# One matmul fewer for the sum of phi(k): a fold on GpSimd, and one more FFN chunk in the output banks

## The chip, the cores and the metric

The kernel runs on one core of one Trainium2 chip. The metric is the device time of one execution in microseconds (us). A time below is a median of several executions, all of them with a granted TensorE clock of 0.998 to 1.000. The span of a profile is some 1.7 us shorter than the time that is reported for the same execution.

Engines are called as in the profile: PE is TensorE, PEld its weight loads, DVE VectorE, ACT ScalarE, POOL GpSimd, SP the queue that issues the DMAs.

## The reference

A gate mixes a linear-attention block (A) and a SwiGLU block (B) of the same tokens. 2048 tokens, width 512, 32 heads of 16, FFN width 1376, bf16 inputs and output.

```python
def _A_ref(x, wqkv, wo):
    ...                                            # q, k, v: 32 heads of 16
    phi = lambda t: jnp.where(t > 0, t + 1, jnp.exp(t)) + 1e-6
    pq, pk = phi(q), phi(k)
    kv = jnp.einsum("bhsd,bhse->bhde", pk, v)
    z = jnp.einsum("bhsd->bhd", pk)                # the sum of phi(k) over the tokens
    num = jnp.einsum("bhqd,bhde->bhqe", pq, kv)
    den = jnp.einsum("bhqd,bhd->bhq", pq, z)[..., None] + 1e-6
    o = num / den
    return ... @ wo
...
g = _sigmoid((x * gate_w).sum(-1, keepdims=True))
return g * a + (1 - g) * b                         # b = (silu(x w1) * (x w3)) w2
```

The change touches `z`: 512 numbers, each a sum over 2048 tokens, which the kernel needs on all 128 partitions.

## The kernel before

Tokens lie on the partitions, 128 at a time, in 16 tiles. For each tile of k the kernel forms phi(k) and GpSimd adds it to `pks` (128x512, fp32), so that `pks` holds 128 partial sums per column. What remains is to sum over the partitions and to give the result to all of them. A matmul with a matrix of ones does both. Its inputs are bf16, so GpSimd first splits `pks` into a high bf16 part and a low one (what the rounding to bf16 left over), and two products add up in one bank.

```python
    nc.gpsimd.tensor_add(pks[:], pks[:], pk_sb[:, t, :])        # 15 times (L194)
    ...
    for tt in range(TPB - 1):                                   # q of block 0, and the last XP products
        emit_q(0, tt, psM, "mm")
        emit_xp(n_xp + tt, XP_ps)
    ...                                                         # XP_sb copies, last q, rem, kvT
    pks_hi = consts.tile([P, D], BF16, name="pks_hi")
    nc.gpsimd.tensor_copy(pks_hi[:], pks[:])                    # L421
    pks_lo = consts.tile([P, D], BF16, name="pks_lo")
    nc.gpsimd.tensor_sub(pks_lo[:], pks[:], pks_hi[:])          # L423
    for fc in range(FC):
        emit_ffn(0, fc)
        if fc == 0:
            z_ps = psX.tile([P, D], FP32, tag="XP1", name="z_ps")
            nc.tensor.matmul(z_ps[:], lhsT=ones_b[:], rhs=pks_hi[:], start=True, stop=False)   # L428
            nc.tensor.matmul(z_ps[:], lhsT=ones_b[:], rhs=pks_lo[:], start=False, stop=True)   # L429
            nc.scalar.activation(out=z_sb[:], in_=z_ps[:], func=ACT.Copy)
        if 1 <= fc <= TPB:
            emit_den(0, fc - 1)                                 # GpSimd: qz = pq * z_sb (L225)
        ...
```

PSUM has two pools: `psM`, a ring of four banks that nearly everything uses, and `psX`, four single banks XP0 to XP3. An FFN chunk takes two banks of the ring, one for gate and one for up. Chunk 4 of block 0 already goes aside to XP2 and XP3.

```python
    def emit_ffn(tb, fc):
        ...
        aside = tb == 0 and fc == 4
        gate_ps = (psX if aside else psM).tile([P, TB], FP32, tag="XP2" if aside else "mm", ...)
        ...  # four products L310
        up_ps = (psX if aside else psM).tile([P, TB], FP32, tag="XP3" if aside else "mm", ...)
        ...  # four products L318, then ACT tanh, DVE gs (L325), DVE hT (L328)

    def phi(dst, ps):
        e_ins = nc.scalar.activation(out=e[:], in_=ps, func=ACT.Exp)              # L140
        nc.vector.tensor_scalar(out=em[:], in0=e[:], scalar1=1.0, scalar2=1e-6,
                                op0=ALU.min, op1=ALU.add)                         # L142 phi_m
        nc.vector.scalar_tensor_tensor(out=dst, in0=ps, scalar=0.0, in1=em[:],
                                       op0=ALU.max, op1=ALU.add)                  # L145
```

The order of the instructions on PE is fixed by the program.

## Time and profile before

| | before |
|---|---|
| time, first 3 runs | 180.53 us (180.15 to 180.85) |
| span of the profile | 178.7 us |
| PE busy | 174.1 us, 97% |
| DVE, ACT, POOL busy | 67%, 37%, 34% |

The head of the page of the kernel before: span, busy time by engine, and the first line of the chain that ended last.

```profile
span 178.7 us, 2472 instructions
...
PE 174.1 (97%) x877; PEld 84.6 (47%) x893; DVE 119.3 (67%) x205; ACT 66.6 (37%) x126; POOL 61.3 (34%) x69
...
PE 97%; issue 1%; DVE 0%; DVEq 0%
```

A busy PE may still wait between products, so its waits count for more. This is the whole list of PE's waits in the kernel before (who waited for whom: us in total, times, longest):

```profile
PE warm L161 <- PEq L471: 0.8, 1, 0.8
```

One wait, at the start. Now PE around the place of the change, from the timeline of the kernel before (start, duration, engine, line, operation). A line is a group; its duration runs to the end of its last product.

```profile
39.94 0.81 PE L318 MATMUL up_ps<-xT,w_sb 128*128 128x512 bf16 x3
40.59 0.38 PE L428 MATMUL z_ps<-pks_hi,ones_b 128*128 128x512 bf16 x1
40.80 0.38 PE L429 MATMUL z_ps<-pks_lo,ones_b 128*128 128x512 bf16 x1
41.02 1.03 PE L310 MATMUL gate_ps<-xT,w_sb 128*128 128x512 bf16 x4
41.88 1.03 PE L318 MATMUL up_ps<-xT,w_sb 128*128 128x512 bf16 x4
```

The durations are 0.38 us a product, the starts are 0.22 us apart: 40.59, 40.80, 41.02. The products overlap in the pipeline, and the spacing of the starts is what one of them costs in a stream. The same view on POOL and on DVE (idle time and its releaser in brackets):

```profile
34.49 0.61 POOL L421 CAST pks_hi<-pks 128x512 bf16<-128x512 f32 x1
35.18 1.16 POOL L423 TENSOR_TENSOR pks_lo<-pks,pks_hi 128x512 bf16<-128x512 f32 x1
38.95 1.05 POOL L254 TENSOR_TENSOR hr<-upr,gsr 128x192 bf16<-128x192 f32 x2 [2.61 <-DVE cl L258]
41.89 4.54 POOL L225 TENSOR_TENSOR qz<-pq,z_sb 128x512 f32<-128x512 bf16 x4 [1.89 <-ACT z_sb L430]
```

```profile
37.61 0.28 DVE L142 TENSOR_SCALAR phi_m<-phi_e 128x512 bf16<-128x512 bf16 x1
37.92 0.69 DVE L145 SCALAR_TENSOR_TENSOR pq<-q_ps,phi_m 128x512 bf16<-128x512 f32 x1
...
43.09 0.69 DVE L228 TENSOR_REDUCE den<-qz 128x32 f32<-128x512 f32 x1 [1.05 <-POOL qz L225]
```

POOL has split `pks` by 36.34 (35.18 + 1.16), four microseconds before z is due, and then waits for DVE. DVE shows no such wait until 42.04 (the end of the instruction that is cut here), and then waits 1.05 us, until 43.09.

### The profile page before, as it was taken

What the parts mean: (1) busy time and instruction counts of PE and PEld (TensorE: products, weight loads), DVE (VectorE), ACT (ScalarE), POOL (GpSimd) and SP (SyncE); (2) the same over time, 40 slices, a digit from 0 to 9 for tenths busy, and PEclk for the clock granted to TensorE, in tenths of its full rate; (3) what the DMA queues carried; (4) which work ended last, traced back from release to release, by engine and by line L of the source; (5) the groups of instructions that cost most, each with busy time, mean ns of one, the idle gap of its engine ahead of it and who ended that gap; (6) DMA issues with size and microseconds to landing.
All of it is one profiled execution on the core that took longest, in us unless ns stands there. A gap on an engine that the chain in (4) does not pass through costs nothing.

```text
span 178.7 us, 2472 instructions
## 1 busy us (share of the span) xinstructions
PE 174.1 (97%) x877; PEld 84.6 (47%) x893; DVE 119.3 (67%) x205; ACT 66.6 (37%) x126; POOL 61.3 (34%) x69
## 2 busy tenths in 40 slices
PE   8999999999999999999999999999999999999993
PEld 4444444474444545444454544444545444444463
DVE  1588867997998837398786375978754669776000
ACT  3642323476533333342433333342433323341221
POOL 5187575736353323262003232620032328100000
PEclk9999999999999999999999999999999999999999
DMA  5999999901005010124000111240001023300011
GB/s 178 263 272 245 267 321 369 321 6 28 9 12 107 0 48 29 44 55 92 0 4 6 38 37 37 59 93 2 0 7 59 14 62 64 61 0 0 29 44 50
DMA packets 29085, 14.88 MB, mean 83 GB/s; under 512 B 19632, under 2 KB 28816, under 8 KB 29072
## 3 DMA queue, kind: packets, MB, share of 16 engines
q1 hardware_dynamic: 28800, 14.46, 30.2%
q10 hardware_dynamic: 272, 0.26, 0.5%
q8 instruction: 7, 0.11, 0.3%
q14 instruction: 6, 0.05, 0.1%
HBM read 8.42 MB, written 2.10 MB: 59 GB/s over the span
## 4 chain that ended last, share of the span: by engine, by line
PE 97%; issue 1%; DVE 0%; DVEq 0%
PE o_ps L355 19%; PE gate_ps L310 19%; PE up_ps L318 19%; PE o_ps L346 8%; PE q_ps L217 8%; PE XP L204 8%; PE k_ps L184 6%; PE r_ps L241 3%; PE k L184 2%; PE o_ps L350 2%; PE warm L161 2%; PE xTp L174 1%; PE kvT_ps L411 1%; PE W_ps L438 0%; DVE o_out L364 0%
## 5 line engine op out<-in xcount | busy, mean ns | idle before, releaser
L310 PE MATMUL gate_ps<-xT,w_sb 128*128 128x512 bf16 x156 | 40.7, 379 | 0.2
L318 PE MATMUL up_ps<-xT,w_sb 128*128 128x512 bf16 x156 | 40.5, 379 | 0.2
L225 POOL TENSOR_TENSOR qz<-pq,z_sb 128x512 f32<-128x512 bf16 x16 | 18.5, 1165 | 60.3 <-DVE pq L145 58.4
L323 ACT ACTIVATE th<-gate_ps 128x512 bf16<-128x512 f32 x40 | 23.9, 597 | 38.1 <-PE gate_ps L310 36.6
L355 PE MATMUL o_ps<-w_sb,hT 128*128 128x512 bf16 (+2 forms) x176 | 37.3, 354 | 0.2
L325 DVE SCALAR_TENSOR_TENSOR gs<-th,gate_ps 128x512 bf16<-128x512 bf16 x40 | 27.3, 684 | 5.8 <-ACT th L323 5.3
L328 DVE TENSOR_TENSOR hT<-up_ps,gs 128x512 bf16<-128x512 f32 x40 | 27.6, 691 | 3.8
L142 DVE TENSOR_SCALAR phi_m<-phi_e 128x512 bf16<-128x512 bf16 x32 | 15.2, 475 | 18.9 <-ACT phi_e L140 18.8
L355 PEld LDWEIGHTS <-hT 128*128 128x128 bf16 x180 | 16.8, 97 | 17.9
L318 PEld LDWEIGHTS <-w_sb 128*128 128x128 bf16 x160 | 15.6, 98 | 18.9
L310 PEld LDWEIGHTS <-w_sb 128*128 128x128 bf16 x160 | 15.6, 98 | 18.7
L360 ACT ACTIVATE o_out<-o_ps,omg 128x512 bf16<-128x512 f32 (+2 forms) x17 | 11.2, 656 | 30.4 <-PE o_ps L355 30.4
L290 POOL TENSOR_TENSOR pqn<-pq,rden 128x512 bf16<-128x512 bf16 x16 | 16.6, 1057 | 14.0 <-DVE rden L283 11.7
L194 POOL TENSOR_TENSOR pks<-pks,pk_sb 128x512 f32<-128x512 f32 x15 | 17.3, 1155 | 8.1 <-DVE pk_sb L145 7.5
L228 DVE TENSOR_REDUCE den<-qz 128x32 f32<-128x512 f32 x16 | 11.0, 684 | 9.0 <-POOL qz L225 8.9
L346 PE MATMUL o_ps<-W_sb,pqT 128*128 128x512 bf16 (+2 forms) x71 | 16.5, 355 | 0.1
L217 PE MATMUL q_ps<-wq_sb,xT 128*128 128x512 bf16 x63 | 16.4, 379 | 0.1
L204 PE MATMUL XP<-pk_sb,x_sb 128*128 128x512 bf16 x62 | 16.0, 379 | 0.1
L140 ACT ACTIVATE phi_e<-k_ps 128x512 bf16<-128x512 f32 x12 | 7.2, 597 | 14.4 <-PE k_ps L184 12.2
L140 ACT ACTIVATE phi_e<-q_ps 128x512 bf16<-128x512 f32 x16 | 9.6, 597 | 7.8 <-PE q_ps L217 6.7
L184 PE MATMUL k_ps<-wk_sb,xT 128*128 128x512 bf16 x48 | 12.3, 379 | 0.1
L145 DVE SCALAR_TENSOR_TENSOR pq<-q_ps,phi_m 128x512 bf16<-128x512 f32 x16 | 11.1, 691 | 0.5
(59 smaller groups left out, 119.5 us busy)
## 6 DMA issues: line engine op xcount, KB each, us to landing
w_sb<-in_B_w_dram SPq DMA_DIRECT2D x6, 640.0 KB, 8.5
out_dram<-o_out SPq DMA_DIRECT2D x15, 128.0 KB, 1.7
x_sb<-in_A_x_dram SPq DMA_DIRECT2D x3, 512.0 KB, 4.4
x_sb<-in_A_x_dram SPq DMA_DIRECT2D x2, 256.0 KB, 3.5
wq_sb<-in_A_wqkv_dram SPq DMA_DIRECT2D x1, 512.0 KB, 6.6
wv_sb<-in_A_wqkv_dram SPq DMA_DIRECT2D x1, 512.0 KB, 6.5
wo_sb<-in_A_wo_dram SPq DMA_DIRECT2D x1, 512.0 KB, 9.5
wk_sb<-in_A_wqkv_dram ACTq DMA_DIRECT2D x1, 256.0 KB, 3.7
```

What stands on the lines that cost most here:

```text
L184: nc.tensor.matmul(k_ps[:], lhsT=xT[:, kc, t * P : (t + 1) * P], rhs=wk_sb[:, kc, :], start=(kc == 0), stop=(kc == KC - 1),)
L194: nc.gpsimd.tensor_add(pks[:], pks[:], pk_sb[:, t, :])
L204: nc.tensor.matmul(XP_ps[dc][:], lhsT=x_sb[:, t, dc * P : (dc + 1) * P], rhs=pk_sb[:, t, :], start=(t == 0), stop=(t == NT - 1),)
L217: nc.tensor.matmul(q_ps[:], lhsT=xT[:, kc, ts_tok], rhs=wq_sb[:, kc, :], start=(kc == 0), stop=(kc == KC - 1),)
L225: nc.gpsimd.tensor_tensor(out=qz[:], in0=st[tb, "pq"][:, tt, :], in1=z_sb[:], op=ALU.mult)
L310: nc.tensor.matmul(gate_ps[:], lhsT=w1_sb[:, kc, fsl], rhs=xT[:, kc, tok_sl], start=(kc == 0), stop=(kc == KC - 1),)
L318: nc.tensor.matmul(up_ps[:], lhsT=w3_sb[:, kc, fsl], rhs=xT[:, kc, tok_sl], start=(kc == 0), stop=(kc == KC - 1),)
L323: nc.scalar.activation(out=th[:], in_=gate_ps[:], func=ACT.Tanh, scale=0.5)
L325: nc.vector.scalar_tensor_tensor(out=gs[:], in0=th[:], scalar=1.0, in1=gate_ps[:], op0=ALU.add, op1=ALU.mult)
L328: nc.vector.tensor_tensor(out=st[tb, "hT"][:, fc, :], in0=up_ps[:], in1=gs[:], op=ALU.mult)
L346: nc.tensor.matmul(o_ps[:], lhsT=st[tb, "pqT"][:, c, tsl], rhs=W_sb[:, c, a:b], start=(c == 0), stop=False,)
L355: nc.tensor.matmul(o_ps[:], lhsT=st[tb, "hT"][:, fc, tsl], rhs=w2_sb[:, fc, a:b], start=False, stop=(fc == FC - 1),)
```

## The change

The intent is one product for z in place of two. GpSimd adds partitions 64-127 of `pks` onto 0-63. That leaves 64 rows, and the 128 rows of one product hold both parts: the high parts on partitions 0-63, the low parts on 64-127. The fold is emitted earlier in the program than the split was. The second part moves chunk 6 of block 0 out of the ring, to XP0 and XP1, to loosen the ring for a DVE that may be later.

```diff
-        aside = tb == 0 and fc == 4
+        aside = {4: ("XP2", "XP3"), 6: ("XP0", "XP1")}.get(fc) if tb == 0 else None
         gate_ps = (psX if aside else psM).tile(
-            [P, TB], FP32, tag="XP2" if aside else "mm", name="gate_ps"
+            [P, TB], FP32, tag=aside[0] if aside else "mm", name="gate_ps"
         )
 ...                                   # the same for up_ps with aside[1]
         emit_xp(n_xp + tt, XP_ps)
+    HP = P // 2
+    pks_up = consts.tile([HP, D], FP32, name="pks_up")
+    nc.gpsimd.tensor_copy(pks_up[:], pks[HP:P, :])
+    nc.gpsimd.tensor_add(pks[0:HP, :], pks[0:HP, :], pks_up[:])
+    pks_hl = consts.tile([P, D], BF16, name="pks_hl")
+    nc.gpsimd.tensor_copy(pks_hl[0:HP, :], pks[0:HP, :])
+    nc.gpsimd.tensor_sub(pks_hl[HP:P, :], pks[0:HP, :], pks_hl[0:HP, :])
 ...
-    pks_hi = consts.tile([P, D], BF16, name="pks_hi")
-    nc.gpsimd.tensor_copy(pks_hi[:], pks[:])
-    pks_lo = consts.tile([P, D], BF16, name="pks_lo")
-    nc.gpsimd.tensor_sub(pks_lo[:], pks[:], pks_hi[:])
 ...
-            nc.tensor.matmul(z_ps[:], lhsT=ones_b[:], rhs=pks_hi[:], start=True, stop=False)
-            nc.tensor.matmul(z_ps[:], lhsT=ones_b[:], rhs=pks_lo[:], start=False, stop=True)
+            nc.tensor.matmul(z_ps[:], lhsT=ones_b[:], rhs=pks_hl[:], start=True, stop=True)
```

More of the change, by code (lines that the diff above doesn't have):

```diff
@@ L314, in emit_ffn @@
         up_ps = (psX if aside else psM).tile(
-            [P, TB], FP32, tag="XP3" if aside else "mm", name="up_ps"
+            [P, TB], FP32, tag=aside[1] if aside else "mm", name="up_ps"
         )
```

## The prediction

> **What bounds the kernel now.** TensorE. The page gives PE 174.1 us of a 178.7 us span (97%), and the chain that ended last is 97% PE, 1% issue. The list of waits has one entry for PE, 0.8 us at the very start. In the matmul records, from 5.7 us on, 512-column matmuls start 216 ns apart; single gaps of about 431 ns, some 10 us apart and inside accumulations, are lost records, not stalls. The Trainium skill ("TensorE: Matmul & The Clock Gate", section "Wait — 56ns, not 53.3ns?") gives 215.7 ns for this spacing; the trace agrees, so the 379 ns "mean of one" is latency, not what a matmul costs in the stream. The granted clock is 1.0. PE never waits for a tile around the place that changes (34 to 58 us).
>
> **What the change removes and adds.**
> - PE: one 128x512 matmul of z is gone (the timeline shows z at 40.59 and 40.80, the next gate at 41.02). Worth one spacing: 0.216 us. In the listings of both programs nothing else moves on PE, and nothing on VectorE, ScalarE or the DMA queue.
> - Pool: before, a cast of 0.61 us (34.49) and a subtraction of 1.16 us, ended at 36.34. After: copy, add, cast, subtraction, on 64 partitions but the same 512 columns, so I charge full price: about 0.65 + 1.16 + 0.65 + 1.16 = 3.6 us, ended near 38.1. Pool +1.8 us. The z product starts at 40.59: 2.5 us to spare. Pool's next work (hr at 38.95) also starts after that.
> - The FFN chunk fc=6 of block 0 goes to the two idle banks. XP0 and XP1 were last used by W_ps and read by 44.3; chunk 6 starts at 50.5. The next user (q of block 1, 57.4) comes three chunks later. It loosens a ring of four banks on which PE never waits, so it gains nothing.
>
> **Side effect.** VectorE's bf16 tensor_scalar (phi_m) takes 0.28 us, but 0.6 to 1.06 where a Pool instruction runs. "SBUF — State Buffer", "Who interferes with whom", says the two share a port pair and the one that came second blocks; the trace fits. So the phi_m at 37.61 should wait for Pool's last subtraction, near 38.1, and put VectorE back about 0.5 us until its idle 1.05 us at 43.1. The matmul that meets it is up_ps of chunk 0 at 39.72, which needs the bank that the last phi of q leaves at 38.61, now about 39.1: still in time by 0.6. The second W product at 42.75 needs kvT_sb, now about 40.6. No PE stall.
>
> **Sum.** 180.53 - 0.22 = 180.3 us. The three runs before spread over 0.7 us, three times the gain, so within 2% is almost sure, and the sign itself is only likely.
>
> **What would show each step.** PE one matmul fewer; gate of chunk 1 starting 0.22 us after z, and everything behind it 0.22 us earlier; the PE waits still only the one at the start; Pool's fold ended by about 38.1; phi_m near 37.6 lengthened; qz's first start at about 41.7 instead of 41.89; span about 178.5.
>
> **What would make it wrong.** Pool's copy from partitions 64-127 to 0-63, or the subtraction written to 64-127, being much slower than the same-partition forms (over 2.5 us more in all stalls z and with it PE, one for one); VectorE being held up longer than 0.6 us by it, so that up_ps of chunk 0 waits; a hidden stall in PE that the lost records cover, which the two extra banks would free.
>
> I give 0.01 to faster by over 2%, 0.98 to within 2%, 0.01 to slower. Range 179.8 to 180.8 us.

## The result

| | before | after |
|---|---|---|
| time, 6 runs each, same rounds | 180.62 us (180.15 to 180.96) | 180.08 us (179.75 to 180.26) |
| ratio of the fast runs, 95% interval | | 0.9971 (0.9951 to 0.9991) |
| span of the profile | 178.7 us | 178.4 us |

A ratio here is the mean time of one kernel's fast runs over that of the other's fast runs of the same rounds, so it is not quite the ratio of the medians. The first measurement is a gain of 0.5 us, more than twice the forecast of 0.22 us, with an interval from 0.2 to 0.9 us that just holds the forecast. All outputs are right.

The profile after, in the same views. The head of the page, then the whole list of PE's waits:

```profile
span 178.4 us, 2473 instructions
...
PE 173.6 (97%) x876; PEld 84.5 (47%) x892; DVE 119.8 (67%) x205; ACT 66.6 (37%) x126; POOL 63.2 (35%) x71
...
PE 96%; DMA 2%; issue 1%; DVE 0%; DVEq 0%
```

```profile
PE warm L161 <- PEq L473: 0.8, 1, 0.8
PE xTp L174 <- DMA x_sb<-in_A_x_dram: 0.2, 1, 0.2
```

PE has one product fewer and POOL two instructions and 1.9 us more. The only new wait of PE is for the first load of x, at 4 us, which the change does not touch. Then PE, POOL and DVE of the kernel after around the change:

```profile
39.88 0.81 PE L318 MATMUL up_ps<-xT,w_sb 128*128 128x512 bf16 x3
40.52 0.38 PE L431 MATMUL z_ps<-pks_hl,ones_b 128*128 128x512 bf16 x1
40.74 1.03 PE L310 MATMUL gate_ps<-xT,w_sb 128*128 128x512 bf16 x4
41.60 1.03 PE L318 MATMUL up_ps<-xT,w_sb 128*128 128x512 bf16 x4
```

```profile
34.42 0.61 POOL L400 COPY pks_up<-pks 64x512 f32<-64x512 f32 x1
35.11 1.26 POOL L401 TENSOR_TENSOR pks<-pks,pks_up 64x512 f32<-64x512 f32 x1
36.44 0.60 POOL L403 CAST pks_hl<-pks 64x512 bf16<-64x512 f32 x1
37.12 1.15 POOL L404 TENSOR_TENSOR pks_hl<-pks,pks_hl 64x512 bf16<-64x512 f32 x1
39.56 1.05 POOL L254 TENSOR_TENSOR hr<-upr,gsr 128x192 bf16<-128x192 f32 x2 [1.28 <-DVE cl L258]
41.62 4.54 POOL L225 TENSOR_TENSOR qz<-pq,z_sb 128x512 f32<-128x512 bf16 x4 [1.01 <-ACT z_sb L432]
```

```profile
37.65 0.78 DVE L142 TENSOR_SCALAR phi_m<-phi_e 128x512 bf16<-128x512 bf16 x1
38.46 0.69 DVE L145 SCALAR_TENSOR_TENSOR pq<-q_ps,phi_m 128x512 bf16<-128x512 f32 x1
...
42.81 0.69 DVE L228 TENSOR_REDUCE den<-qz 128x32 f32<-128x512 f32 x1 [0.44 <-POOL qz L225]
```

Gate of chunk 1 now starts 0.22 us after z rather than 0.43. Against before it starts 0.28 us earlier (41.02 to 40.74), and 0.06 of that was there already at up_ps (39.94 to 39.88). POOL's fold ends at 38.27 (37.12 + 1.15), two microseconds ahead of z. The phi_m at 37.65 takes 0.78 us; it ends at 38.43, in the records 0.15 us after the end of POOL's last subtraction.

To take the random part out, I use one more number: the **stretch**, from the start of the first XP product to the start of the last o_ps product, taken from the start times of the matmul records in ns. It leaves out the head, before XP, and the tail. In the timelines its two ends are these groups, of before and of after (the last product is the tenth of its group):

```profile
8.98 1.03 PE L204 MATMUL XP<-pk_sb,x_sb 128*128 128x512 bf16 x4
...
175.07 0.72 PE L355 MATMUL o_ps<-w_sb,hT 128*128 128x128 bf16 x10
```

```profile
8.91 1.03 PE L204 MATMUL XP<-pk_sb,x_sb 128*128 128x512 bf16 x4
...
174.79 0.72 PE L355 MATMUL o_ps<-w_sb,hT 128*128 128x128 bf16 x10
```

From the records the stretch is 166.591 us before and 166.378 us after: 0.213 us less. The head (start of the first XP product) went from 8.977 to 8.914 us, and the tail (last product to the end of the span) from 3.115 to 3.119. So the two spans differ by 0.213 + 0.063 - 0.004 = 0.272 us.

### The profile page after: what moved, and what is told of

Its sections match the earlier page's. It is cut to its first block, busy times and chain, and to the rows that moved or that the text cites. A ratio compares the mean times of both kernels' runs of the same rounds, so it can differ in the third digit from the quotient of the medians.

```text
span 178.4 us, 2473 instructions
## 1 busy us (share of the span) xinstructions
PE 173.6 (97%) x876; PEld 84.5 (47%) x892; DVE 119.8 (67%) x205; ACT 66.6 (37%) x126; POOL 63.2 (35%) x71
## 4 chain that ended last, share of the span: by engine, by line
PE 96%; DMA 2%; issue 1%; DVE 0%; DVEq 0%
PE gate_ps L310 19%; PE o_ps L355 19%; PE up_ps L318 19%; PE q_ps L217 8%; PE o_ps L346 8%; PE XP L204 8%; PE k_ps L184 6%; PE r_ps L241 3%; PE o_ps L350 2%; PE k L184 2%; DMA x_sb<-in_A_x_dram 2%; PE xTp L174 1%; PE kvT_ps L418 1%; PE W_ps L440 0%; DVE o_out L364 0%
## 5 line engine op out<-in xcount | busy, mean ns | idle before, releaser
L142 DVE TENSOR_SCALAR phi_m<-phi_e 128x512 bf16<-128x512 bf16 x32 | 15.7, 490 | 18.9 <-ACT phi_e L140 18.8
```

## The experiments

Theory A: PE never waits behind the head, so the change is worth one matmul spacing and nothing else. Rival B: more was won, by the two banks or in some other place, as the first ratio of 0.9971 suggests. A second question is how near POOL and DVE came to costing something.

| run | stretch, us | ratio to before (95%) | median of its runs, us |
|---|---|---|---|
| before (first profile) | 166.591 | | |
| after (first profile) | 166.378 | 0.9971 (0.9951 to 0.9991) | 180.08 |
| e0_after_again | 166.377 | 0.9989 (0.9970 to 1.0008) | 180.12 |
| e1_fold_only | 166.377 | 0.9986 (0.9969 to 1.0004) | 180.06 |
| e2_aside_only | 166.592 | 0.9997 (0.9983 to 1.0012) | 180.35 |
| e3_hi_only | 166.377 | 0.9990 (0.9968 to 1.0012) | 180.13 |
| e4_nine_products | 168.103 | 1.0094 (1.0065 to 1.0122) | 182.27 |
| e5_pool_plus2 | 166.376 | 0.9987 (0.9950 to 1.0023) | 180.33 |
| e6_pool_plus6 | 168.228 | 1.0078 (1.0051 to 1.0104) | 181.90 |
| e7_long_op | 166.873 | 1.0020 (0.9996 to 1.0044) | 180.81 |
| e8_two_ops | 166.378 | 0.9988 (0.9965 to 1.0010) | 180.10 |

Runs e0 to e3 shared one chip and its runs of before, as did e4 to e6, and e7 and e8.

### e0_after_again: the control

No edit.

> The changed kernel again, as the control for the other runs of this call. My theory (A): TensorE never waits, so the change is worth the one matmul of z that is gone, 0.216 us; ratio to before about 0.9988, and in the trace 0.213 us less from the first XP product to the last o_ps product (166.591 us before, 166.378 in the first profile of after). Rival (B): the 0.5 us of the first measurement is real, so something beyond that matmul was won (the two output banks free a hidden wait, or the head is shorter); ratio about 0.997 again.

Ratio 0.9989, stretch 166.377 us. The gain of 0.5 us did not come back. Theory A's 0.9988 lies within both intervals, that of the first measurement too. By the times alone this run does not decide, as its interval begins at 0.9970; what the later runs say together stands under "The measured time".

### e1_fold_only: the fold without the banks

```diff
-        aside = {4: ("XP2", "XP3"), 6: ("XP0", "XP1")}.get(fc) if tb == 0 else None
+        aside = {4: ("XP2", "XP3")}.get(fc) if tb == 0 else None
```

> Fold and single z product, but chunk 6 stays in the four-bank ring. Theory A: all of the gain is here; 166.378 us from first XP to last o_ps product as in after, time within 0.1 us of e0. Rival B (banks): the gain is smaller than that of e0, and with VectorE half a microsecond late PE should show waits for a bank in chunks 1 to 6, longer stretch by 0.1 us or more.

166.377 us, ratio 0.9986, and PE's waits are the one at the start. All of the gain is in the fold, and the ring of four banks holds without the second part of the change, even with the later DVE.

### e2_aside_only: the banks without the fold

```diff
-        aside = tb == 0 and fc == 4
+        aside = {4: ("XP2", "XP3"), 6: ("XP0", "XP1")}.get(fc) if tb == 0 else None
```

(and `aside[0]`, `aside[1]` for the tags, as in the change.)

> The kernel before with only chunk 6 moved to the two output banks; two z products. Theory A: nothing; 166.59 us from first XP to last o_ps product, ratio 1.000. Rival B (banks): 0.2 to 0.3 us faster than before.

166.592 us against 166.591, ratio 0.9997. The second part of the change does nothing. With e1 this takes rival B's banks away.

### e3_hi_only: one product without a fold

```diff
     nc.gpsimd.tensor_copy(pks_hi[:], pks[:])
-    pks_lo = consts.tile([P, D], BF16, name="pks_lo")
-    nc.gpsimd.tensor_sub(pks_lo[:], pks[:], pks_hi[:])
 ...
-            nc.tensor.matmul(z_ps[:], lhsT=ones_b[:], rhs=pks_hi[:], start=True, stop=False)
-            nc.tensor.matmul(z_ps[:], lhsT=ones_b[:], rhs=pks_lo[:], start=False, stop=True)
+            nc.tensor.matmul(z_ps[:], lhsT=ones_b[:], rhs=pks_hi[:], start=True, stop=True)
```

> The kernel before with the low part dropped: one z product of the bf16 cast of all 128 partitions, no fold, Pool shorter by 1.16 us rather than longer by 1.9. Theory A: same PE gain as after, 166.38 us for the stretch, ratio about 0.9988; VectorE's phi_m near 37.6 back to 0.28 us. The result should still pass against the reference, since rounding errors of 128 partial sums average out. If Pool's extra 1.9 us in after costs anything, this run is faster than e0 by it.

166.377 us and correct. The same phi_m on DVE, in this run:

```profile
37.58 0.29 DVE L142 TENSOR_SCALAR phi_m<-phi_e 128x512 bf16<-128x512 bf16 x1
```

Back to 0.29 us. POOL does three microseconds less than in the change (one cast of 0.61 us against a fold from 34.42 to 38.27), DVE half a microsecond less, and the time is the same. This is the simplest kernel with the gain. It gives up the low part of z; the comparison with the reference still passes, and I did not measure how much of its tolerance that takes.

### e4_nine_products: the price of a product

```diff
-            nc.tensor.matmul(z_ps[:], lhsT=ones_b[:], rhs=pks_hl[:], start=True, stop=True)
+            for _ in range(9):
+                nc.tensor.matmul(z_ps[:], lhsT=ones_b[:], rhs=pks_hl[:], start=True, stop=True)
```

> The changed kernel with the z product made nine times into the same bank (each overwrites the last, the result stays right). Eight more than after, seven more than before. Theory A: each costs its spacing of 0.216 us and nothing hides it: the stretch from first XP to last o_ps product 166.378 + 8 x 0.216 = 168.1 us, time about 1.5 us over before (ratio 1.008). If z lay in slack of PE, the time would not move; if one product cost its 0.379 us of latency, 3.0 us over after.

168.103 - 166.378 = 1.725 us for eight more products, each with its own weight load (900 loads in the trace against 892), 0.2156 us each. In time, the ratio to before is 1.0094, about 1.7 us, where 168.103 - 166.591 = 1.5 us (1.0084) was due; the interval holds it. Here the effect is large enough for the times themselves to show it. The price is neither nothing nor the 0.379 us of one product's duration.

### e5_pool_plus2 and e6_pool_plus6: how much later may the fold be?

Copies in place on POOL between the addition and the cast, 2 in e5 and 6 in e6; the result does not change. The cut shows e6; e5 has `range(2)`.

```diff
+    for _ in range(6):
+        nc.gpsimd.tensor_copy(pks[0:HP, :], pks[0:HP, :])
     nc.gpsimd.tensor_copy(pks_hl[0:HP, :], pks[0:HP, :])
```

> The changed kernel with two more Pool copies of 64x512 in the fold (in place, result unchanged), about 0.69 us each. Fold ends near 39.65 instead of 38.27, z starts at 40.52. Theory A: still in time; stretch 166.38 us, no change to after. If the fold has less slack than the 2.25 us I read from the trace, PE shows a wait before z.

> The changed kernel with six more Pool copies in the fold, about 4.1 us: the fold ends near 42.4, past z's slot. Theory A: PE waits before z until about 42.5, some 1.9 to 2.0 us, one for one from the end of the slack of about 2.2 us; time 1.9 us over after (ratio to before about 1.0095). If part of it is won back later, PE would have had to have slack behind z, which theory A denies.

e5: 166.376 us, nothing lost. e6: PE waits. Two lines of PE's timeline in e6:

```profile
39.39 1.03 PE L318 MATMUL up_ps<-xT,w_sb 128*128 128x512 bf16 x4
42.11 0.38 PE L433 MATMUL z_ps<-pks_hl,ones_b 128*128 128x512 bf16 x1 [1.69 <-POOL pks_hl L406]
```

The idle time in brackets counts from the modelled end of the product before; counted in starts, z came 1.86 us later than its place in the stream, and the stretch is longer by that to within 0.01 us: 168.228 - 166.378 = 1.850 us. The expectation was 1.9 to 2.0. The six copies put the fold off by 4.03 us (36.19 to 40.22 in the timeline of e6), so 4.03 - 1.85 = 2.18 us of slack were there. Nothing was won back behind it. The time agrees: 1.0078, with 168.228 - 166.591 = 1.64 us over before (1.0091) inside the interval.

### e7_long_op and e8_two_ops: how late may DVE be?

Both leave the low part at zero and put other POOL work, which nothing on PE needs, where the last subtraction was. e7 has one addition of 64x1024 into scratch, e8 two of 64x512.

```diff
-    nc.gpsimd.tensor_sub(pks_hl[HP:P, :], pks[0:HP, :], pks_hl[0:HP, :])
+    nc.gpsimd.tensor_tensor(                                            # e7
+        out=scr[:], in0=scr[:],
+        in1=pks_hl[0:HP, None, :].to_broadcast([HP, 2, D]), op=ALU.add,
+    )
+    for j in range(2):                                                  # e8, in its place
+        nc.gpsimd.tensor_tensor(
+            out=scr[:, j, :], in0=scr[:, j, :], in1=pks_hl[0:HP, :], op=ALU.add
+        )
```

(`scr`, a 64x2x512 fp32 tile, and the upper half of `pks_hl` are set to zero early by POOL. The added lines shift the line numbers of these two kernels by 5: L147 is the phi_m that is L142 above.)

> The changed kernel with the low part left at zero (as correct as hi_only), and in the place of Pool's last subtraction (1.15 us) one Pool addition of 64x1024 into scratch, about 2.3 us, from about 37.1 to 39.4. Nothing that PE needs depends on it. Claim to test: VectorE's phi_m near 37.65 is blocked for the whole Pool instruction, until about 39.4 instead of 38.4, so the last phi of q ends near 40.1 to 40.4 and up_ps of chunk 0, due at 39.66 on the same bank, waits 0.5 to 0.8 us: stretch from first XP to last o_ps product about 167.0 to 167.2 us instead of 166.38. My prediction said VectorE has 0.6 us to spare beyond the change; rival: VectorE has more slack than I read, or is only slowed and not blocked, and the stretch stays at 166.38 us.

> The same Pool work as in the run before, cut into two additions of 64x512, about 1.15 us each, one right behind the other. If the lock is held per instruction, phi_m gets in after the first, near 38.3, up_ps of chunk 0 is in time as in after, and the stretch is 166.38 us. If Pool's second addition goes ahead of the waiting phi_m, it is as late as in the run before.

POOL, DVE and PE in e7:

```profile
37.73 2.12 POOL L408 TENSOR_TENSOR scr<-scr,pks_hl 64x1024 f32<-64x1024 f32 x1
```

```profile
38.26 1.75 DVE L147 TENSOR_SCALAR phi_m<-phi_e 128x512 bf16<-128x512 bf16 x1
40.04 0.69 DVE L150 SCALAR_TENSOR_TENSOR pq<-q_ps,phi_m 128x512 bf16<-128x512 f32 x1
```

```profile
39.42 1.03 PE L315 MATMUL gate_ps<-xT,w_sb 128*128 128x512 bf16 x3
40.79 0.38 PE L323 MATMUL up_ps<-xT,w_sb 128*128 128x512 bf16 x1 [0.34 <-DVE pq L150]
```

A POOL instruction whose result PE does not read makes PE wait, by way of DVE: the phi_m takes 1.75 us and ends at 40.01, 0.16 us after POOL's addition (37.73 + 2.12 = 39.85), the last phi of q ends at 40.73, and up_ps of chunk 0, which needs its bank, starts at 40.79. (All of e7 lies some 0.6 us later than after, as its head is longer: the first XP product starts at 9.54 us.) The stretch is 166.873 us, 0.495 more than after. The phi_m was 0.97 us longer than after's 0.78, so DVE had 0.97 - 0.50 = 0.47 us to spare beyond the change. The wait is at the low end of the 0.5 to 0.8 us that I expected, and the stretch is shorter than the expected 167.0 to 167.2 us by 0.13 us, a miss in size; POOL's addition took 2.12 us rather than 2.3.

The same POOL and DVE in e8:

```profile
37.08 2.31 POOL L409 TENSOR_TENSOR scr<-scr,pks_hl 64x512 f32<-64x512 f32 x2
```

```profile
37.60 0.78 DVE L147 TENSOR_SCALAR phi_m<-phi_e 128x512 bf16<-128x512 bf16 x1
38.42 0.69 DVE L150 SCALAR_TENSOR_TENSOR pq<-q_ps,phi_m 128x512 bf16<-128x512 f32 x1
```

POOL is as long at work, but phi_m ends at 38.38, 0.15 us after the first of the two additions (37.08 to 38.23 in the records), while the second is at work, and the stretch is 166.378 us. So this phi_m is held for the rest of the POOL instruction that runs, not for as long as POOL has work. Nor is every DVE instruction held: the pq at 38.42, which reads PSUM, takes 0.69 us in the middle of the second addition, as it does in the kernel before with POOL idle (37.92).

## Why the prediction was right

That the time fell into the range says little: the range of 1 us also holds the 180.53 us of the kernel before. The mechanism is tested by the stretch and the experiments.

**The bound and the price of the product.** The prediction said PE never waits and the product is worth its spacing, 0.216 us. The stretch shows 0.213 us, e4 0.2156 us for each of eight more, and e5 and e8 the same 166.38 us with quite different work on POOL. Six runs with one product and nothing else added to PE's path (after, e0, e1, e3, e5, e8) have stretches of 166.376 to 166.378 us, the two with two products 166.591 and 166.592. The Trainium skill ("TensorE: Matmul & The Clock Gate", "Wait — 56ns, not 53.3ns?") gives 215.7 ns for this spacing; the trace agrees.

**The banks.** "It gains nothing": e1 and e2 show that.

**POOL.** I charged 3.6 us and an end near 38.1; the fold took 3.85 us and ended at 38.27. The term left out was the gaps of about 0.08 us between instructions that wait for each other, and the addition took 1.26 rather than 1.16 us. Crossing partitions cost nothing that shows: the copy from 64-127 to 0-63 took 0.61 us, and the copies of the same 64x512 fp32 in place in e5 and e6 took 0.60 to 0.62 us. The slack of 2.5 us in the prediction was 2.2 us by e6.

**DVE.** The phi_m was to wait near 38.1 and put DVE back by 0.5 us: it took 0.78 us instead of 0.28, and DVE's idle time before the first den shrank from 1.05 to 0.44 us. The Trainium skill ("SBUF — State Buffer", "Who interferes with whom") gives as the cause a port pair that DVE and GpSimd share: for a DVE instruction in a mode that uses two ports, which it says `tensor_scalar` can enter, who issues first gets the pair for the whole instruction, and the other is blocked. The trace agrees, with e3 (0.29 us), after and e8 (0.78 us) and e7 (1.75 us) as the measure: the held phi_m ends 0.15 to 0.16 us after the POOL instruction that ran when it started. The runs show the hold and when it ends; that ports are the reason is the page's account. The 0.6 to 1.06 us in the prediction is too narrow: over the whole kernel before, a phi_m that starts while POOL runs takes 0.37 to 1.16 us, depending on how much of the POOL instruction is left. The spare 0.6 us before up_ps of chunk 0 was 0.47 us.

**The measured time.** 180.08 us lies in the range of 179.8 to 180.8, 0.2 us under the forecast. Where do the other 0.3 us of the first measurement come from? Not from the change, as far as the runs tell: five more runs with one product give ratios of 0.9986 to 0.9990, mean 0.9988, which is 0.22 us of 180.4. Each of their intervals still holds 1. Together they say more: the 18 executions of e0, e1 and e3 are on average 0.20 us faster than the 11 of before on the same chip, with a standard error of 0.11 us by their scatter (an estimate), so that 0.22 us fits and 0.5 us does not. In the two profiles 0.06 us lie in the head. The head differs from run to run by more than the whole gain: over the eleven profiles the first XP product starts between 8.65 us (e6) and 9.82 us (e5), in heads whose PE instructions are the same. The same group of six k products in e6, then in e5 (where it starts 0.43 us later, after a wait of 0.3 us for the first load of x):

```profile
4.57 1.63 PE L184 MATMUL k<-wk_sb,xT 128*128 128x512 bf16 x6
```

```profile
5.00 2.37 PE L184 MATMUL k<-wk_sb,xT 128*128 128x512 bf16 x6
```

In the records the starts are 0.427 us apart at first and 0.216 later; the change comes during the first of these six products in e6 and during the fifth in e5. So the step to full rate comes at another moment in each run. I did not take the head of each timed run apart, so that the surplus of the first measurement lay in the heads is an argument, not shown. That it is not in the stretch is shown for the two profiled executions, and the stretches repeat to 0.002 us from run to run.

## What to carry to other kernels

When one engine works without a wait, a change is worth the spacing that it takes out of that engine's stream, times the count, and neither the duration in the profile nor work that moves elsewhere; check with the list of waits and with the starts of the records. Spare time on the other engines has an end that can be measured: put dummy work in until the bound engine waits, and remember that a long GpSimd instruction reaches PE through VectorE although no data goes that way. Where the gain is a tenth of a per cent, compare a stretch of the trace that leaves out the head, since the times alone need many runs to see it.

## What the Trainium skill lacked or had wrong

- "TensorE: Matmul & The Clock Gate", section "Back-to-back issue gap", gives about 131 ns per 512-column matmul in a sustained stream with weight loads and says that the longer formula over-counts there. Here, in a stream with a weight load for each product, 665 of the 835 spacings in the stretch of before are 215 or 216 ns, and eight more products cost 0.2156 us each. The 215.7 ns of the page's first part are right.
- "GPSIMD Engine Reference", section 5.1, says that in ordinary elementwise operations every core works on its own 16 partitions. It does not say what an operation costs that reads partitions 64-127 and writes 0-63: here 0.61 us for a 64x512 fp32 copy, no more than the same copy on its own partitions (0.60 to 0.62 us in e5 and e6). Nor that half the partitions take no less time: 0.60 us for a 64x512 cast where 128x512 took 0.61, 1.15 us for the 64x512 subtraction where 128x512 took 1.16.
- "SBUF — State Buffer", section "Who interferes with whom", has the block, but not how it looks in a profile: as a longer VectorE instruction (0.28 us becoming 0.78 or 1.75), not as idle time before it, so it is in no list of waits. It does not say either that VectorE gets in between two GpSimd instructions queued back to back; e8 shows that it does here.
- "TensorE: Matmul & The Clock Gate", section "What you observe", puts the step to full rate at about 4 us of sustained activity, 0.5 us to either side. Here PE starts at 0.84 us and the step comes in the product that starts at 4.57 us in e6 and in one that starts at 6.67 us in e7, 3.7 and 5.8 us later, with no wait of PE between in either: a spread of two microseconds. In e8 it comes near 3.95 us, after 3.1 us. The page's next section, "What's actually happening", is nearer to this: it reports 6, 11 or 14 slow products for one and the same kernel.
